# Softmax split over three engines, fewer fill-in products and operands built chunk by chunk in a fused attention and feed-forward kernel

## The chip, the cores and the metric

The kernel runs on 1 core of one Trainium2 chip. The metric is the device time of one launch in microseconds. All operands are 32-bit floats in memory.

## What is computed

The reference is sparse attention, then a mixture of 8 experts with Sinkhorn-balanced weights, then a feed-forward block with an ELU. Only the attention and the first product of the experts bear on the change.

```python
B, H, S, D = 4, 8, 576, 64; stride = 32
scores = q @ k.T / sqrt(D)                       # per batch and head
mask_local   = (rel >= 0) & (rel < 32)           # heads 0 to 3
mask_strided = (rel >= 0) & (i % 32 == j % 32)   # heads 4 to 7
scores = where(mask, scores, -1e9)
attn = exp(scores - max(scores)); attn /= sum(attn) + 1e-9
x = (attn @ v)  as  (B*S, H*D) = (2304, 512)
P = sinkhorn(exp(x @ w_gate - max))              # 8 iterations
for e in range(8): out += P[:, e] * (relu(x @ w1[e]) @ w2[e])
result = elu(out @ w_in) @ w_out
```

## The kernel before, in words

**Attention.** Heads are taken in pairs, batch by batch: 16 pairs `m`, and each pair in two halves, so 32 units `u`. A unit is one score tile set: 5 or 4 tiles of 128x96 in a pair of local heads, 6 or 5 tiles of 108x54 in a pair of strided heads. The order of pairs in a batch is local, strided, local, strided. A unit passes four stages, which are generators in `attention()` (L683). `att_s1` (L415) transposes q and k by chunks on PE; ACT copies q into the block operand `q_blk` (L437), DVE copies k into `kT` (L443). `att_s2` (L453) has the score products (L470), the mask add on DVE (L484), the maximum on DVE (L487); the exponentials (L491, one activation per tile, each with the tile's row sum) and the normalisation (L495 to L497: two small DVE operations, then a multiplication on POOL, GpSimd's row in the profile) are put off. `att_s3` (L503) transposes the weights on PE (L511), and DVE or ACT copies them to `eT` (L514, L516). `att_s4` (L519) multiplies by v (L529) and DVE copies the result to x (L549).

**Order.** The kernel writes the order of each engine's instructions by hand. In one round of `attention()` the stages of several units are called in the order s2(u), s1, s4(u-3), s1, s3(u-2), s3(u-2), and after each call `tick()` counts down the operations that are put off: `DEF_EXP = 3` and `DEF_NORM = 5` say after how many calls. After a call in the first stage one step of a build (`build_step`) or of the weights' preparation (`prep_step`) is issued too. Each engine runs its instructions in that order.

**Fill-in products.** While attention runs alone, `warm_up` (L337) adds a 128x512 product of constants (L341) to the first nine PSUM banks and then to every second one (`WARM_MOD = 2`). Its result is overwritten.

**First operands.** The experts' first product runs on 1024 tokens by a scheme of seven products (Strassen-Winograd). Its seven right operands are B11, B21 (`build_a`, L247) and T2, T1, T3, T4, B22 (`build_b`, L255), each of 2 chunks of 128 rows by 512 tokens, each split into a high and a low part: ACT casts the high one, DVE or POOL subtracts for the low one (`low`, L167). T1 to T4 are differences that DVE takes first (L267). `build_a` starts when batch 0 is done and `build_b` when batch 1 is done (`batch_done`, L634), each with both chunks.

**Where attention alone ends.** At round 21 (`MOE_FROM`) the experts' first product (`gemm1`, L969, products at L925) begins on PE, and the rest of attention is spread between its steps. `need` (L678) issues the rest of a build that a product needs. The gate (`gate_block`, L577, products L589) waits in PE's order for the same operands. From about 230 us to the end at 2067 us the kernel is the experts' products (L925, L1074).

Of the kernel before, what the change touches and what calls it, by code (L numbers as in the profile page):

```python
# [24 lines left out]
KD = DM // P  # L25
# [50 lines left out]
def sparse_attention_moe_kernel(ctx: ExitStack, tc: tile.TileContext, a, out):  # L76
# [170 lines left out]
    def build_a(src):  # L247

        hi, lo = xb
        for x, c0 in ((B11, 0), (B21, 2)):  # L250
            yield from splits([(hi[:, x, c], lo[:, x, c], src(c + c0), ve if c else po_) for c in (0, 1)])
            built.add(x)
            yield True

    def build_b(a, b, home=None):  # L255


        hi, lo = xb

        def minus(x, y, i, c):  # L260
            if home:
                out = home(i, c)
            elif i == 4:
                out = y
            else:
                out = hp_.tile([P, HALF], F32, tag="hh" if c else "hl", name="t")
            ve.tensor_tensor(out=out, in0=x, in1=y, op=ALU.subtract)  # L267
            return out

        t1 = [minus(b(c), a(c), 1, c) for c in (0, 1)]  # L270
        yield True
        t2 = [minus(b(c + 2), t1[c], 2, c) for c in (0, 1)]
        yield True

        def both(x, t, engs):
            for c in (0, 1):
                se.copy(hi[:, x, c], t[c])
            yield True
            for c in (0, 1):
                low(hi[:, x, c], lo[:, x, c], t[c], engs[c])  # L280
            built.add(x)
            yield True

        yield from both(T2, t2, (ve, ve))
        yield from both(T1, t1, (ve, po_))
        t3 = [minus(t2[c], a(c), 3, c) for c in (0, 1)]
        yield from both(T3, t3, (ve, po_))

        t4 = [minus(a(c + 2), t2[c], 4, c) for c in (0, 1)]
        yield from both(T4, t4, (ve, po_))  # L290
        b22 = [b(c + 2) for c in (0, 1)]
        yield from both(B22, b22, (ve, ve))
# [160 lines left out]
    def att_s2(u):  # L453
# [11 lines left out]
        for i, x in enumerate(tiles):  # L465
            if local:
                qc, kc = x * P, max(0, x * LQ - STRIDE)
            else:
                qc, kc = x * 2 * NJ, x * NJ
            pe.matmul(  # L470
                pp[:nq, i * nk : (i + 1) * nk],
                q_blk[m % 2][:, qc : qc + nq],
                t["kT"][:, kc : kc + nk],
                start=True,
                stop=True,
            )
# [10 lines left out]
        ve.tensor_reduce(out=ng, in_=e, axis=AX.X, op=ALU.max, negate=True)  # L487

        def exps():
            for i in range(nt):  # L490
                se.activation(e[:, i], e[:, i], AF.Exp, bias=ng[:, i : i + 1], accum_out=sm[:, i : i + 1])  # L491

        def norm():
            rc = st_p.tile([P, 6], F32, tag="rc", name="rc")[:nq, :nt]
# [8 lines left out]
    def att_s3(u):  # L503
# [3 lines left out]
        for i0 in (0, 3):  # L507
# [5 lines left out]
            if i0 and not local:  # L513
                se.copy(dst, pt[:nk, : n * nq])  # L514
            else:
                ve.tensor_copy(dst, pt[:nk, : n * nq])  # L516
# [60 lines left out]
    def gate_block():  # L577

        for half, parts in enumerate((((B11, 0), (B21, 2)), ((B11, 0), (T1, 0), (B22, 2)))):
            while not all(x in built for x, _ in parts):  # L580
                yield True
# [52 lines left out]
    def batch_done(b):  # L634

        if b == 0:
            po_.tensor_copy(x1_[:, :, : S - HALF], x0_[:, :, HALF:])
            start_build((0, False, "a"), build_a(lambda c: x0_[:, c, :HALF]))
            gates.append(gate_block())
        elif b == 1:  # L640
            start_build((0, False, "b"), build_b(lambda c: x0_[:, c, :HALF], lambda c: x1_[:, c, :HALF]))
            gates.append(gate_tile(NA // P, x1_[:, :, HALF:]))

    def pair_done(m):

        b, hp = pair_of(m)
        t0 = max(NA, b * S)
# [30 lines left out]
    def need(x):  # L678
        while x not in built:
# [3 lines left out]
    def attention():  # L683
# [4 lines left out]
        for u in range(NU + 5):  # L688
# [5 lines left out]
            if u - 5 == 2 * H:  # L694
                batch_done(1)
# [19 lines left out]
            if w == H - 1:  # L715
                batch_done(0)
# [252 lines left out]
    def gemm1(sg, p, early=False):  # L969
# [6 lines left out]
        def prod(dst, wi, xi, start=True):  # L976
            need(xi)
            for c in products(dst, w, xb, wi, xi, start=start):
# [311 lines left out]
WARM0, WARM1, WARM_MOD, WARM_OF, WARM_N = 14, 10, 2, 1, 512  # L1290
QK_BUFS = 3
DEF_EXP, DEF_NORM = 3, 5
# [35 lines left out]
```

## Time and profile before

| | |
|---|---|
| median of 3 runs | 2068.71 us (2067.12 to 2068.77) |
| profiled execution, its own time | 2068.94 us |
| its span | 2067.2 us |
| TensorE (PE) busy | 2029.2 us, 98% |
| VectorE (DVE), ScalarE (ACT), GpSimd (POOL) busy | 1306.3, 743.4, 633.8 us |
| mean granted clock of TensorE | 0.989 |

The profile's times are microseconds from the span's start. The profiled execution's own time stands 1.7 us over its span, and 0.2 us over the median. A busy PE need not be at its full rate: PEclk is the share of the full clock (2.4 GHz) that was granted, so 0.50 is 1.2 GHz. In a timeline, the first number is the start, the second the length, and brackets give the idle time ahead of it with what ended it. Matmuls overlap, so the distance between two starts is the price of one, not its length.

### The profile page before, as it was taken

The page shows a single profiled execution, that of the slowest core. Times are in us where ns is not written, and L with a number is a line of the kernel's source. Part 1 is how long each engine was busy: PE and PEld are TensorE (multiplying, and loading weights), DVE is VectorE, ACT ScalarE, POOL GpSimd, SP SyncE. Part 2 cuts the span into 40 slices and gives each one's busy share as a digit, 9 for nine tenths or more (in the row PEclk, how much of TensorE's full clock was granted, in tenths as well). Part 3 has the DMA queues.
Part 4 walks back from the last instruction along what each step waited for, and adds up shares of the span by engine and source line. Part 5 has one row for each costly group of instructions (what it writes and reads, how often), then busy time and mean ns, then how long its engine had stood idle before and what let it go on. Part 6 is the DMA issues. An engine that isn't in the chain of part 4 may idle for free.

```text
span 2067.2 us, 26959 instructions
## 1 busy us (share of the span) xinstructions
PE 2029.2 (98%) x10196; PEld 1681.0 (81%) x10196; DVE 1306.3 (63%) x2165; ACT 743.4 (36%) x1707; POOL 633.8 (31%) x709
## 2 busy tenths in 40 slices
PE   9889999999999999999999999999999989999999
PEld 7767778888888888788888888888888878887887
DVE  6767766555555546566666676766665475558665
ACT  7656233223222323322222222222222254445543
POOL 2422333333332324322222222222222222224240
PEclk9899999999999999999999999999999999999999
DMA  9632111111111113222222222222221101122111
GB/s 195 132 72 73 68 52 61 41 52 62 52 41 52 61 51 101 73 83 81 75 84 72 84 75 80 79 74 85 72 77 46 42 21 42 41 82 92 42 51 51
DMA packets 143378, 143.12 MB, mean 69 GB/s; under 512 B 67328, under 2 KB 106128, under 8 KB 143248
## 3 DMA queue, kind: packets, MB, share of 16 engines
q1 hardware_dynamic: 142288, 141.20, 23.0%
q8 instruction: 80, 1.31, 0.3%
q14 instruction: 50, 0.41, 0.1%
q10 hardware_dynamic: 960, 0.21, 0.1%
HBM read 123.55 MB, written 20.19 MB: 70 GB/s over the span
## 4 chain that ended last, share of the span: by engine, by line
PE 90%; DVE 5%; ACT 4%; issue 1%; POOL 0%; DVEq 0%; ACTq 0%; POOLq 0%
PE ybank L1074 46%; PE bank L925 39%; DVE xl L168 1%; PE ybank L529 1%; ACT g L948 1%; PE bank L470 1%; ACT g L947 1%; DVE u L984 1%; PE ybank L511 1%; ACT e_t L491 1%; PE ybank L470 1%; ACT hh L952 0%; PE bank L425 0%; ACT q_blk L437 0%; DVE rawa L267 0%
## 5 line engine op out<-in xcount | busy, mean ns | idle before, releaser
L1074 PE MATMUL ybank<-w2h,hh 128*128 128x512 f32 x1280 | 502.7, 393 | 1.5 <-ACT q_blk L437 0.8
L1074 PE MATMUL ybank<-w2h,hl 128*128 128x512 f32 x1280 | 498.3, 389 | 0.0
L1074 PE MATMUL ybank<-w2l,hh 128*128 128x512 f32 x1280 | 498.2, 389 | 0.0
L925 PE MATMUL bank<-xh,w1h 128*128 128x512 f32 x1120 | 446.6, 399 | 16.3 <-DVE u L984 7.8
L925 PE MATMUL bank<-xl,w1h 128*128 128x512 f32 x1120 | 440.0, 393 | 6.1 <-DVE xl L168 6.1
L925 PE MATMUL bank<-xh,w1l 128*128 128x512 f32 x1120 | 438.6, 392 | 0.0
L168 POOL TENSOR_TENSOR w1l<-w1raw,w1h 128x256 fp32r<-128x256 f32 x240 | 207.8, 886 | 438.4 <-ACT w1h L158 438.3
L1105 DVE SCALAR_TENSOR_TENSOR acc<-ybank,prob,acc 128x512 f32<-128x512 f32 x244 | 182.7, 749 | 231.4 <-PE ybank L1074 231.0
L1074 PEld LDWEIGHTS ybank<-w2h,hh 128*128 128x128 f32 x1280 | 240.3, 188 | 52.7 <-DVE acc L1091 1.9
L1074 PEld LDWEIGHTS ybank<-w2h,hl 128*128 128x128 f32 x1280 | 240.2, 188 | 50.3
L1074 PEld LDWEIGHTS ybank<-w2l,hh 128*128 128x128 f32 x1280 | 240.4, 188 | 48.1
L168 POOL TENSOR_TENSOR w2l<-w2raw,w2h 128x512 fp32r<-128x512 f32 x80 | 104.1, 1302 | 564.8 <-ACT w2h L158 549.5
L158 ACT CAST w2h<-w2raw 128x512 fp32r<-128x512 f32 x160 | 97.4, 622 | 476.3 <-issue 396.1
L925 PEld LDWEIGHTS bank<-xh,w1h 128*128 128x128 f32 x1120 | 211.8, 189 | 67.0 <-DVE u L984 11.1
L925 PEld LDWEIGHTS bank<-xl,w1h 128*128 128x128 f32 x1120 | 212.1, 189 | 47.0 <-DVE xl L168 7.8
L925 PEld LDWEIGHTS bank<-xh,w1l 128*128 128x128 f32 x1120 | 211.9, 189 | 45.1
L984 DVE TENSOR_TENSOR u<-bank,a 128x512 f32<-128x512 f32 x160 | 110.5, 691 | 194.8 <-PE bank L925 163.5
L186 POOL TENSOR_TENSOR wsum<-w1raw 128x256 f32<-128x256 f32 x160 | 125.3, 783 | 216.0 <-DMA w1raw<-in_moe_w 149.4
L940 ACT ACTIVATE hh<-bank 128x512 fp32r<-128x512 f32 x192 | 114.1, 594 | 106.8 <-DVE bank L984 104.0
L942 DVE SCALAR_TENSOR_TENSOR hl<-bank,hh 128x512 fp32r<-128x512 f32 x192 | 131.3, 684 | 6.3
L168 DVE TENSOR_TENSOR w1l<-wsum,w1h 128x512 fp32r<-128x512 f32 (+1 forms) x164 | 119.2, 735 | 13.7 <-ACT w1h L158 12.7
L940 ACT ACTIVATE hh<-c 128x512 fp32r<-128x512 f32 x64 | 40.6, 634 | 242.7 <-DVE c L984 242.7
(198 smaller groups left out, 2707.1 us busy)
## 6 DMA issues: line engine op xcount, KB each, us to landing
w1raw<-in_moe_w SPq DMA_DIRECT2D x64, 512.0 KB, 3.4
w2raw<-in_moe_w SPq DMA_DIRECT2D x64, 512.0 KB, 3.5
raw<-in_moe_w_in SPq DMA_DIRECT2D x16, 512.0 KB, 3.8
w_conv<-val SPq DMA_DIRECT2D x32, 256.0 KB, 2.5
raw<-in_moe_w_out SPq DMA_DIRECT2D x16, 512.0 KB, 3.7
w1raw<-w_conv SPq DMA_DIRECT2D x16, 512.0 KB
w2raw<-w_conv SPq DMA_DIRECT2D x16, 512.0 KB, 3.4
q_t<-in_q SPq DMA_DIRECT2D x32, 144.0 KB, 3.9
```

What stands on the lines that cost most here:

```text
L158: se.copy(hi, src)
L168: eng.tensor_tensor(out=lo, in0=src, in1=hi.bitcast(F32), op=ALU.subtract)
L186: po_.tensor_tensor(out=o, in0=x, in1=y, op=op)
L470: pe.matmul(pp[:nq, i * nk : (i + 1) * nk], q_blk[m % 2][:, qc : qc + nq], t["kT"][:, kc : kc + nk], start=True, stop=True,)
L491: se.activation(e[:, i], e[:, i], AF.Exp, bias=ng[:, i : i + 1], accum_out=sm[:, i : i + 1])
L511: pe.transpose(pt[:nk, i * nq : (i + 1) * nq], s["e"][:, i0 + i], ident[:nq, :nq])
L925: pe.matmul(dst, a_[:, wi, c, :], b_[:, xi, c, :], start=start and i == 0, stop=stop and i == 5, skip_group_check=True,)
L940: se.activation(hh, src, AF.Relu)
L942: ve.scalar_tensor_tensor(out=hl, in0=src, scalar=0.0, in1=hh.bitcast(F32), op0=ALU.max, op1=ALU.subtract)
L984: ve.tensor_tensor(out=out, in0=x, in1=y, op=ALU.add)
L1074: pe.matmul(y, x[:, cs], w[:, f], start=first and f + m == 0, stop=last and f == 1 and m == 2)
L1105: ve.scalar_tensor_tensor(out=at, in0=y, scalar=prob[:, g, e : e + 1], in1=at, op0=ALU.mult, op1=ALU.add)
```

## The change

The softmax of a unit is spread otherwise. The maximum is kept with its own sign, POOL subtracts it from all tiles in one operation, ACT takes one exponential over all tiles, and DVE sums the rows in the normalisation, which is put off by one more call. ACT makes all copies to `eT`. Fill-in products follow every eighth bank. `build_a` and `build_b` take the chunks one at a time: chunk 0 of `build_a` starts when the second pair of batch 0 is done, chunk 1 with the fourth; the same for `build_b` in batch 1. A product waits for the chunk that it reads.

```diff
-    def build_a(src):
+    def build_a(src, cs=(0, 1)):
...
-            yield from splits([(hi[:, x, c], lo[:, x, c], src(c + c0), ve if c else po_) for c in (0, 1)])
-            built.add(x)
+            yield from splits([(hi[:, x, c], lo[:, x, c], src(c + c0), ve if c else po_) for c in cs])
+            built.update((x, c) for c in cs)
...
-    def build_b(a, b, home=None):
+    def build_b(a, b, home=None, cs=(0, 1)):
...
-        t1 = [minus(b(c), a(c), 1, c) for c in (0, 1)]
+        t1 = {c: minus(b(c), a(c), 1, c) for c in cs}
...
-        ve.tensor_reduce(out=ng, in_=e, axis=AX.X, op=ALU.max, negate=True)
+        ve.tensor_reduce(out=ng, in_=e, axis=AX.X, op=ALU.max)
+        po_.tensor_tensor(out=e, in0=e, in1=ng[:, :, None].to_broadcast([nq, nt, nk]), op=ALU.subtract)
 
         def exps():
-            for i in range(nt):
-                se.activation(e[:, i], e[:, i], AF.Exp, bias=ng[:, i : i + 1], accum_out=sm[:, i : i + 1])
+            se.activation(e, e, AF.Exp)
 
         def norm():
+            ve.tensor_reduce(out=sm, in_=e, axis=AX.X, op=ALU.add)
...
-            if i0 and not local:
-                se.copy(dst, pt[:nk, : n * nq])
-            else:
-                ve.tensor_copy(dst, pt[:nk, : n * nq])
+            se.copy(dst, pt[:nk, : n * nq])
...
-            start_build((0, False, "a"), build_a(lambda c: x0_[:, c, :HALF]))
...
-            start_build((0, False, "b"), build_b(lambda c: x0_[:, c, :HALF], lambda c: x1_[:, c, :HALF]))
...
     def pair_done(m):
 
         b, hp = pair_of(m)
+        if b < 2 and m % 2:
+
+            cs = (m % KD // 2,)
+            if b:
+                start_build("b", build_b(lambda c: x0_[:, c, :HALF], lambda c: x1_[:, c, :HALF], cs=cs))
+            else:
+                start_build("a", build_a(lambda c: x0_[:, c, :HALF], cs))
...
-    def need(x):
-        while x not in built:
+    def need(x, c=0):
+        while (x, c) not in built:
...
-            need(xi)
-            for c in products(dst, w, xb, wi, xi, start=start):
+            work = products(dst, w, xb, wi, xi, start=start)
+            for c in (0, 1):
+                need(xi, c)
+                next(work)
                 if c == 0:
                     gap()
...
-WARM0, WARM1, WARM_MOD, WARM_OF, WARM_N = 14, 10, 2, 1, 512
+WARM0, WARM1, WARM_MOD, WARM_OF, WARM_N = 14, 10, 8, 1, 512
...
-DEF_EXP, DEF_NORM = 3, 5
+DEF_EXP, DEF_NORM = 3, 6
```

In the order of instructions this looks as follows at three places. First DVE, one round in the middle of attention alone (`e_t` are a unit's scores, `ng` the maxima, `sm` the row sums, `rc` their inverse, `acc` holds x), before:

```order
L484 TENSOR_TENSOR e_t<-bank,m_local 128x384
L487 TENSOR_REDUCE ng<-e_t 128x4
L549 COPY acc<-ybank 128x18x18
L443 COPY kT<-bank 128x9x32
L516 COPY eT<-ybank 54x324
L495 TENSOR_SCALAR rc<-sm 128x4
L496 RECIPROCAL rc<-rc 128x4
```

and with the change:

```order
L479 TENSOR_TENSOR e_t<-bank,m_local 128x384
L482 TENSOR_REDUCE ng<-e_t 128x4
L489 TENSOR_REDUCE sm<-e_t 128x5
L491 TENSOR_SCALAR rc<-sm 128x5
L492 RECIPROCAL rc<-rc 128x5
L542 COPY acc<-ybank 128x18x18
L443 COPY kT<-bank 128x9x32
```

The copy to `eT` has gone to ACT; the normalisation is now that of the unit before (128x5 behind the maximum of 128x4) and has a sum of its own.

Second PE, the same stretch of attention alone, before:

```order
L529 MATMUL ybank<-eT,v_t 64x64 x10
L425 MATMUL bank<-ident,k_t 128x96 x3
L341 MATMUL ybank<-warm 128x512
L511 MATMUL ybank<-ident,e_t 96x128 x4
L341 MATMUL bank<-warm 128x512
L470 MATMUL bank<-kT,q_blk_110 128x96 x5
L425 MATMUL bank<-ident,q_t 128x96 x3
L341 MATMUL ybank<-warm 128x512
L529 MATMUL ybank<-eT,v_t 64x64 x8
```

and with the change:

```order
L522 MATMUL ybank<-eT,v_t 64x64 x10
L425 MATMUL bank<-ident,k_t 128x96 x3
L507 MATMUL ybank<-ident,e_t 96x128 x4
L471 MATMUL bank<-kT,q_blk_110 128x96 x5
L425 MATMUL bank<-ident,q_t 128x96 x3
L341 MATMUL ybank<-warm 128x512
L522 MATMUL ybank<-eT,v_t 64x64 x8
```

Two of three fill-in products are gone here; over the whole stage there are 21 in place of 60 (the 14 at the very start stay).

Third DVE around the first product of the experts, whose first mask add from a `ybank` marks the place (`t` are the differences of `build_b`, `xl` the low parts), before:

```order
L484 TENSOR_TENSOR e_t<-ybank,m_str 108x270
L487 TENSOR_REDUCE ng<-e_t 108x5
L267 TENSOR_TENSOR t<-acc 128x512 x2
L267 TENSOR_TENSOR t<-acc,t 128x512 x2
L549 COPY xlate<-ybank 128x320
L443 COPY kT<-ybank 128x288
L168 TENSOR_TENSOR xl<-t,xh 128x512 x2
```

and with the change:

```order
L479 TENSOR_TENSOR e_t<-ybank,m_str 108x270
L482 TENSOR_REDUCE ng<-e_t 108x5
L489 TENSOR_REDUCE sm<-e_t 108x6
L491 TENSOR_SCALAR rc<-sm 108x6
L492 RECIPROCAL rc<-rc 108x6
L267 TENSOR_TENSOR t<-acc 128x512
L267 TENSOR_TENSOR t<-acc,t 128x512
L542 COPY xlate<-ybank 128x320
L443 COPY kT<-ybank 128x288
L168 TENSOR_TENSOR xl<-t,xh 128x512
```

Only chunk 1 is left here. Chunk 0 of `build_b`, 4 differences and 5 low parts on DVE, has moved ahead, into the last rounds of attention alone.

## Rows read from the trace of the kernel before

**Rows 1.** The page's 40 slices: PE's busy time in tenths.

```profile
PE   9889999999999999999999999999999989999999
```

**Rows 2.** Busy time by engine in five stretches: us, PE, PEld, DVE, ACT, POOL, PEclk, DMA.

```profile
20.59:54.00 33.41, 32.95 (x397) 28.48 (x395) 26.19 (x71) 27.84 (x116) 8.51 (x12) 1.00 1.03 201
...
30.05:45.02 14.97, 14.75 (x181) 12.72 (x177) 11.71 (x32) 12.31 (x51) 3.20 (x5) 1.00 0.94 213
...
54.00:90.42 36.42, 33.32 (x310) 28.66 (x308) 25.82 (x59) 26.32 (x98) 14.43 (x17) 0.77 0.58 120
...
62.84:77.97 15.13, 15.13 (x100) 13.01 (x99) 7.86 (x19) 8.40 (x39) 4.37 (x5) 0.50 0.63 127
...
90.42:147.94 57.52, 49.21 (x334) 34.25 (x331) 40.71 (x83) 30.55 (x100) 21.20 (x20) 0.91 0.44 94
```

**Rows 3.** PE's timeline: fill-ins at either clock, and starts after idle time.

```profile
15.98 1.70 PE L470 MATMUL bank<-kT,q_blk 128*108 128x54 f32 x12 [2.26 <-ACT q_blk L437]
...
30.05 0.47 PE L425 MATMUL bank<-ident,k_t 96*128 96x96 f32 x3
...
38.72 0.48 PE L341 MATMUL bank<-warm 128*128 128x512 f32 x1
39.04 1.25 PE L470 MATMUL bank<-kT,q_blk 128*128 128x96 f32 x10
...
61.38 1.53 PE L529 MATMUL ybank<-eT,v_t 54*64 54x54 f32 x24 [2.16 <-DVE eT L516]
...
71.59 0.78 PE L341 MATMUL bank<-warm 128*128 128x512 f32 x1
72.16 1.91 PE L470 MATMUL bank<-kT,q_blk 128*108 128x54 f32 x10
...
102.54 0.50 PE L925 MATMUL bank<-xl,w1h 128*128 128x512 f32 x1 [1.91 <-DVE xl L168]
...
118.16 0.50 PE L925 MATMUL bank<-xl,w1h 128*128 128x512 f32 x1 [2.26 <-DVE xl L168]
```

**Rows 4.** DVE by line and shape, 0 to 90.42 us: count, busy us, mean ns.

```profile
L516 DVE COPY eT<-ybank 96x384 f32<-96x384 f32 x8 | 4.4, 554 | 2.1 <-PE ybank L511 1.6
...
L487 DVE TENSOR_REDUCE ng<-e_t 128x5 f32<-128x480 f32 x5 | 3.3, 655 | 0.2
...
L487 DVE TENSOR_REDUCE ng<-e_t 108x5 f32<-108x270 f32 x4 | 1.7, 436 | 0.1
...
L516 DVE COPY eT<-ybank 96x128 f32<-96x128 f32 x4 | 1.1, 278 | 0.0
```

**Rows 5.** ACT's timeline at unit 0: the first of its five exponentials, then `q_blk`.

```profile
12.59 0.38 ACT L491 ACTIVATE e_t<-e_t,ng 128x96 f32<-128x96 f32 x1
...
14.52 1.36 ACT L437 ACTIVATE q_blk<-bank 64x288 f32<-64x288 f32 x2
```

**Rows 6.** ACT by line and shape, 0 to 90.42 us: casts of 512 and of 256 elements.

```profile
L158 ACT CAST xh<-acc 128x512 fp32r<-128x512 f32 x4 | 2.5, 616 | 0.0
...
L158 ACT CAST w1h<-wsum 128x256 fp32r<-128x256 f32 x4 | 1.6, 397 | 0.0
```

**Rows 7.** POOL by line and shape, 0 to 90.42 us: largest and smallest multiplication.

```profile
L497 POOL TENSOR_TENSOR e_t<-e_t,rc 128x480 f32<-128x480 f32 x5 | 5.0, 990 | 24.5 <-DVE rc L496 14.0 <-ACT eT L514 7.4 <-DVE e_t L484 3.1
...
L497 POOL TENSOR_TENSOR e_t<-e_t,rc 108x270 f32<-108x270 f32 x4 | 2.6, 640 | 11.2 <-DVE rc L496 5.4 <-PE bank L470 3.8 <-ACT xh L158 1.9
```

**Rows 8.** Timelines of POOL (first and last of four operations in a row) and DVE.

```profile
56.18 1.27 POOL L168 TENSOR_TENSOR xl<-acc,xh 128x512 fp32r<-128x512 f32 x1
...
58.78 0.74 POOL L186 TENSOR_TENSOR wsum<-w1raw,wsum 128x256 f32<-128x256 f32 x1
...
56.68 3.39 DVE L168 TENSOR_TENSOR xl<-acc,xh 128x512 fp32r<-128x512 f32 x1
```

**Rows 9.** Line 168 on DVE, 0 to 240 us: min/median/max ns.

```profile
L168 DVE TENSOR_TENSOR xl<-t,xh x5: 681/693/1222, 97.4 to 112.0; 128x512 fp32r<-128x512 f32 x5
```

**Rows 10.** PE's waits, 90 to 320 us: total us, times, longest.

```profile
PE bank L925 <- DVE xl L168: 6.1, 5, 2.3
```

More of the change, by code (lines that the diff above doesn't have):

```diff
@@ L268, in minus @@
             return out
-        t1 = [minus(b(c), a(c), 1, c) for c in (0, 1)]
+        t1 = {c: minus(b(c), a(c), 1, c) for c in cs}
         yield True
-        t2 = [minus(b(c + 2), t1[c], 2, c) for c in (0, 1)]
+        t2 = {c: minus(b(c + 2), t1[c], 2, c) for c in cs}
         yield True
         def both(x, t, engs):
-            for c in (0, 1):
+            for c in cs:
                 se.copy(hi[:, x, c], t[c])
             yield True
-            for c in (0, 1):
+            for c in cs:
                 low(hi[:, x, c], lo[:, x, c], t[c], engs[c])
-            built.add(x)
+                built.add((x, c))
             yield True
@@ L285, in build_b @@
         yield from both(T1, t1, (ve, po_))
-        t3 = [minus(t2[c], a(c), 3, c) for c in (0, 1)]
+        t3 = {c: minus(t2[c], a(c), 3, c) for c in cs}
         yield from both(T3, t3, (ve, po_))
-        t4 = [minus(a(c + 2), t2[c], 4, c) for c in (0, 1)]
+        t4 = {c: minus(a(c + 2), t2[c], 4, c) for c in cs}
         yield from both(T4, t4, (ve, po_))
-        b22 = [b(c + 2) for c in (0, 1)]
+        b22 = {c: b(c + 2) for c in cs}
         yield from both(B22, b22, (ve, ve))
@@ L469, in att_s2 @@
                 qc, kc = x * 2 * NJ, x * NJ
[L470 to L476, printed above, removed]
+            dst = pp[:nq, i * nk : (i + 1) * nk]
+            pe.matmul(dst, q_blk[m % 2][:, qc : qc + nq], t["kT"][:, kc : kc + nk], start=True, stop=True)
         s3 = pp[:nq, : nt * nk].rearrange("p (t k) -> p t k", k=nk)
@@ L579, in gate_block @@
         for half, parts in enumerate((((B11, 0), (B21, 2)), ((B11, 0), (T1, 0), (B22, 2)))):
-            while not all(x in built for x, _ in parts):
+            while not all((x, c) in built for x, _ in parts for c in (0, 1)):
                 yield True
@@ L693, in attention @@
             s2, s3, s4 = of(att_s2, u - 2), of(att_s3, u - 4), of(att_s4, u - 5)
-            if u - 5 == 2 * H:
-                batch_done(1)
             for gen in (s2, s1, s4, s1, s3, s3):
@@ L714, in attention @@
                 reorder_v(u // 8 + 1, H // 4 + RE_IN.index(u % 8))
-            if w == H - 1:
-                batch_done(0)
+            if w == H - 1 or w == 2 * H - 1:
+                batch_done(w // H)
     load_qk(0)
```

## The prediction

> **What bounds it now.** I start with the slices of the page: PE is busy in nearly all of them [rows 1], so only two things can bring time: PE work that disappears, and the few places where PE idles or runs at the lower clock. From about 230 us on the kernel is not touched by the change. So I read the first 150 us by stretches [rows 2]. In 20.59 to 54.00 nine units of attention pass, 33.41/9 = 3.71 us each; PE is busy 32.95 of it at full clock, so PE sets the pace there, although DVE (26.19) and ACT (27.84) are not far below. In 54.00 to 90.42 seven units take 5.2 us each, and the granted clock is 0.77: PE waited 2.16 us ahead of 61.38 [rows 3] and then ran at 0.50 (1.2 GHz) from 62.84 to 77.97. The same piece of program lies between 30.05 and 38.72 at full clock [rows 3]: 8.67 us against 15.13, so the lower clock cost 6.5 us. In 90.42 to 147.94 the experts' first product has begun; PE is busy only 49.21 of 57.52, and the clock is 0.91. What it waited for is above all low parts of its right operands [rows 10], which DVE makes too late.
>
> A look at the idle times ahead of clock losses: 2.26, 2.16 and 2.26 us were followed by the lower clock, 1.91 us was not [rows 3]. [...]
>
> **The change, part by part.** For the softmax I use the steady stretch 30.05 to 45.02, four units in 14.97 us [rows 2].
>
> *PE.* A fill-in at full clock costs 38.72 to 39.04, 0.32 us [rows 3]. In four units there are 24 banks, so 12 fill-ins before and 3 after: 9 x 0.32 = 2.9 us. PE idles 14.97 - 14.75 = 0.2 us here. PE's floor is then 14.97 - 0.2 - 2.9 = 11.9 us, 2.97 a unit.
>
> *DVE.* It loses the copies to `eT`, six in four units, between 0.278 and 0.554 us each [rows 4], some 2.7 us (most are of the longer kinds); it gains four row sums, which read what the maxima read: 0.436 to 0.655 [rows 4], together 2.1. So 11.71 - 2.7 + 2.1 = 11.1 us, 2.8 a unit: below PE, but by little.
>
> *ACT.* Five exponentials with their sums held ACT from 12.59 to 14.50, 1.9 us [rows 5]; four units have 20 of them, at most 7.6 us, and as the strided tiles are narrower I take 7.2. One exponential over 270 to 480 elements isn't in the trace; the nearest rows are casts, 0.397 for 256 and 0.616 for 512 [rows 6], so 0.4 to 0.6, four of them 2.0. With the six copies (about 2.7): 12.31 - 7.2 + 2.0 + 2.7 = 9.8 us. ACT gets room.
>
> *POOL.* The subtraction has the shapes of the multiplication: 0.640 to 0.990 [rows 7], so 3.2 more on 3.20 us [rows 2], 6.4 of 12. It is behind the maximum in POOL's order, and what is queued behind it (weights' low parts, the multiplication of the unit before) waits for that maximum. It lengthens a unit's own chain, but the sum is wanted only a round later, behind the next maximum; there I cost it at nothing. POOL needs 1.27 us for a low part that DVE makes in 0.693 [rows 8, 9]. On DVE the four subtractions would cost about 2.2 us (as the maxima) and raise its floor to 13.3, over PE's. The Trainium skill ("GPSIMD Engine Reference", section 4.1) says that elementwise work belongs on VectorE, GpSimd being about twice as slow for two inputs; the ratio agrees with the rows, and by that rule the stage would end at DVE's 13.3 us; since POOL has the room, the sum goes by POOL.
>
> So a unit is bounded by 2.97 below and today's 3.71 above (the copies to `eT`, the value product and the next transposes follow each other closely, and DVE is nearly full). I take 3.2, nearer to the floor, because PE was 99% busy in the rows with slower neighbours. **Term 1**, nine units: 9 x 3.2 - 33.4 = -4.6 us (0 to -6.7).
>
> **Term 2, the start.** Unit 0's exponentials hold the `q_blk` copies until 14.52 [rows 5], PE waits for them until 15.98 and then has the lower clock for about 4 us [rows 3]. Now POOL's subtraction (0.99) and one exponential (0.6) follow the maximum, which was there before the first exponential at 12.59 [rows 5]: the copies start by 14.2 at the latest, 0.3 us earlier, and up to 0.6 more if the maximum had been there for some time (ACT had come from other copies). I take 0.9. PE also gets there sooner, so its wait may still be near 2 us; the clock I leave as it is (if it holds, -1.7 more). -1 (0 to -2.6).
>
> **Term 3, the last seven units of attention alone** (36.42 us). Here the builds run. PE's floor is 7 x 2.97 = 20.8, but DVE now gets chunk 0 of `build_b`: 4 differences and 5 low parts at about 0.69 [rows 9], 6.2 us. DVE: 25.82 [rows 2] - 1.1 (softmax, 7/4 of 0.6) + 6.2 = 30.9 us, so DVE becomes the engine that sets the pace. With about 2 us of its own waits 33: -3.4 us. Ends: 30.9 (-5.5), and 36.4 (0), about what PE needs if the clock stays at half: without fill-ins the stretch at half clock is 15.13 - 7 x 0.57 [rows 3] = 11.1 us against 8.67 - 7 x 0.32 = 6.4 at full, a factor 1.7, and 7 x 2.97 x 1.7 = 35.
>
> **Term 4, the first product of the experts** (57.52 us). PE idles 8.3 us. The clock's 0.91 is 0.09 x 57.5 x 2 = 10.4 us at half, which cost 10.4 x (1 - 1/1.7) = 4.3. Half of the operands are now there, and each product reads chunk 0 first. DVE has 6.2 us less here. I take 4.5 of the idle time and, as no 2 us wait should be left, 3 of the clock: -7.5 (0 to -12.6). The weights' preparation and the gate stay where they are behind it. What comes after, 13 units between the experts' products, has ACT relieved and POOL loaded, and PE there has no idle time worth a term: 0.
>
> Sum: -4.6 - 1 - 3.4 - 7.5 = -16.5 us on the profiled execution's 2068.94: **2052.4**. The median lies 0.2 lower: 2052.
>
> **Rivals.**
>
> *The clock falls and stays (ends slower).* Fewer fill-ins leave PE with more short waits, DVE and PE being within 0.8 us in four units; one 2 us wait early, and PE runs at 1.2 GHz with little to raise it. A unit is then 2.97 x 1.7 = 5.05 us. In all 17 units from 15.98 on, the experts begin at 102, 11.5 us later than now, and term 4 gives only the 4.5 of idle time: +7, 2076 us. Each of the ten early units at the lower clock costs 1.85 against my 3.2, each of the last seven, which DVE paces, 0.35. So with the last seven and term 4 without their clock it decides from 6 of the ten early units on, and from 8 on the kernel is measurably slower. For it: after 61.38 the clock stayed low for 16 us, with fill-ins. Against: at full clock PE stays the busiest engine, and a 1.91 us wait did no harm.
>
> *DVE waits for POOL.* At 56.68 a low part on DVE took 3.39 us instead of 0.69: it ended when four operations of POOL in a row (56.18 to 59.52) had ended [rows 8], and then PE stood 2.16 us. POOL now has an operation more per unit. Some 24 DVE operations of that kind (2 + 9 + 6 of the builds, 7 of the weights) run until about 130 us; if half of them meet one more subtraction of 0.8 us: +9.6, 2062 us. By the Trainium skill ("SBUF — State Buffer", section "Who interferes with whom") a VectorE instruction with two inputs in SBUF and a GpSimd instruction that reads SBUF exclude each other for a whole instruction, and a reduction never takes part. The trace agrees, and the wait outlasted four instructions, not one; mask adds (one PSUM operand) and sums would be spared.
>
> *The change moves work and wins nothing.* The unit stays at 3.71 because its chain of copies and products sets it, not PE's fill-ins; chunk 0 costs its 6.2 us ahead of the experts' product, and term 4 gives 7.5 back. Start 0. Together -1.3: 2067.6. For it: ACT and DVE had 0.78 to 0.83 of the steady stretch. Against: PE's 99%.
>
> **How the numbers follow.** Forecast (2042 to 2059): 0.62. DVE behind POOL, 2062: 0.18, faster too. Nothing won, 2067.6: 0.10, the same. Clock, 2076: 0.10, of which I give 0.02 to "same" because it may last for fewer units. A measurement tells 0.2%, 4 us, from no change. Faster 0.80, same 0.12, slower 0.08. All terms at their ends give 2041.5; the range goes from 2041 to 2067, which leaves out the clock case and part of the others.
>
> **What the profile would show.** Right: four steady units in 12 to 13 us with PE over 0.9 busy at clock 1.00; the experts' first product at about 81 us instead of 90.4; waits for `xl` there at most half of 6.1 us; DVE fullest in the last rounds before. Wrong: PEclk of 0.5 in several of the first slices; DVE operations of line 168 over 1.5 us; steady units at 3.7 us with PE idle between them; or waits for the subtraction ahead of the exponentials that come through to PE.

## The result, and the profile after

The changed kernel takes 2085.32 us (median of 5 runs, 2081.02 to 2086.54), the kernel before 2068.77 us on the same chip: ratio 1.0073 [1.0056, 1.0091], slower by 0.7%, where 2052 was forecast. Its profiled execution took 2084.83 us, 15.9 more than that of before. From the page, PE's busy time, its slices and its clock:

```profile
PE 2035.8 (98%) x10157; PEld 1691.1 (81%) x10157; DVE 1310.4 (63%) x2149; ACT 717.2 (34%) x1467; POOL 659.5 (32%) x741
...
PE   8789999999999999999999999999999989999999
...
PEclk7679999999999999999999999999999999999999
```

PE is busier than before (2035.8 against 2029.2 us) with 39 products fewer: the same work ran at a lower clock, and the loss lies in the first three slices, some 156 us. Five stretches of the changed kernel by engine (columns as in [rows 2]):

```profile
14.29:108.13 93.84, 78.42 (x691) 71.01 (x692) 62.53 (x137) 46.59 (x102) 37.69 (x46) 0.65 0.64 132
35.77:56.25 20.48, 18.41 (x167) 16.67 (x168) 12.37 (x29) 10.27 (x22) 8.84 (x10) 0.67 0.66 147
56.25:79.28 23.03, 18.41 (x167) 16.67 (x168) 15.53 (x31) 11.25 (x25) 10.07 (x14) 0.65 0.53 112
79.28:102.62 23.34, 19.03 (x168) 17.17 (x168) 17.89 (x38) 12.08 (x28) 9.98 (x12) 0.65 0.37 76
108.13:166.21 58.08, 51.50 (x333) 37.09 (x331) 36.26 (x73) 23.26 (x51) 23.20 (x26) 0.84 0.39 88
```

The experts begin at 108.13 instead of 90.42 us, 17.7 later; the mean clock up to there is 0.65. Their first product takes 58.08 us (57.52 before), and what comes behind it takes 2.4 us less (1916.9 us from 166.21 to the span's end, 1919.3 from 147.94 before). So attention alone holds the whole loss. The second to fourth rows are rounds of four units: the first of them takes 20.48 us, 5.12 a unit, where four units took 14.97 before [rows 2]. Where a round begins is read from PE's timeline, at starts with idle time ahead:

```profile
14.29 2.23 PE L471 MATMUL bank<-kT,q_blk 128*108 128x54 f32 x12 [1.74 <-ACT q_blk L437]
19.83 1.30 PE L507 MATMUL ybank<-ident,e_t 128*96 128x128 f32 x5 [2.33 <-POOL e_t L493]
32.26 0.91 PE L522 MATMUL ybank<-eT,v_t 54*64 54x54 f32 x24 [0.60 <-ACT eT L509]
35.77 2.38 PE L471 MATMUL bank<-kT,q_blk 128*108 128x54 f32 x12 [1.48 <-DVE kT L443]
56.25 2.38 PE L471 MATMUL bank<-kT,q_blk 128*108 128x54 f32 x12 [1.48 <-DVE kT L443]
79.28 2.38 PE L471 MATMUL bank<-kT,q_blk 128*108 128x54 f32 x12 [4.02 <-DVE kT L443]
96.96 1.19 PE L522 MATMUL ybank<-eT,v_t 54*64 54x54 f32 x24 [0.90 <-ACT eT L509]
102.62 2.38 PE L471 MATMUL bank<-kT,q_blk 128*108 128x54 f32 x12 [3.35 <-ACT eT L509]
```

PE waits at the first unit of each strided pair: three times for `kT`, at 14.29 for `q_blk`, at 102.62 for `eT`. And the clock round such a place, in windows of four microseconds:

```profile
32.00:36.00 4.00, 2.25 (x35) 1.89 (x35) 3.52 (x8) 3.00 (x7) 1.98 (x3) 0.87 1.31 244
36.00:40.00 4.00, 4.00 (x36) 3.67 (x36) 1.67 (x4) 0.81 (x2) 0.55 (x1) 0.50 0.21 32
40.00:44.00 4.00, 4.00 (x22) 3.80 (x22) 1.27 (x5) 1.22 (x3) 1.00 (x2) 0.50 0.26 76
44.00:48.00 4.00, 4.00 (x35) 3.66 (x34) 2.57 (x7) 2.40 (x6) 2.60 (x3) 0.50 0.50 113
48.00:52.00 4.00, 4.00 (x46) 3.65 (x45) 2.85 (x7) 2.37 (x4) 0.99 (x1) 0.93 1.05 316
52.00:56.00 4.00, 2.18 (x35) 1.63 (x33) 3.90 (x9) 3.47 (x8) 3.58 (x4) 0.93 1.18 191
```

At 0.50 PE is the bound (4.00 of 4.00) and the others wait for it. When the clock rises, PE runs ahead, DVE is full (3.52, 3.90 of 4.00), PE waits, the clock is 0.50 again. What DVE does just ahead of `kT`, from its timeline, and POOL's subtractions of the same microseconds:

```profile
30.34 0.81 DVE L491 TENSOR_SCALAR rc<-sm 108x5 f32<-108x5 f32 x1
...
32.70 0.55 DVE L482 TENSOR_REDUCE ng<-e_t 128x4 f32<-128x384 f32 x1
33.17 0.64 DVE L489 TENSOR_REDUCE sm<-e_t 128x5 f32<-128x480 f32 x1
33.84 0.43 DVE L491 TENSOR_SCALAR rc<-sm 128x5 f32<-128x5 f32 x1
34.31 0.19 DVE L492 RECIPROCAL rc<-rc 128x5 f32<-128x5 f32 x1
34.41 0.67 DVE L542 COPY acc<-ybank 128x324 f32<-128x324 f32 x1
34.93 0.69 DVE L443 COPY kT<-bank 128x288 f32<-128x288 f32 x1
```

```profile
30.14 0.99 POOL L483 TENSOR_TENSOR e_t<-e_t,ng 128x480 f32<-128x480 f32 x1 [3.92 <-PE bank L425]
...
33.42 0.83 POOL L483 TENSOR_TENSOR e_t<-e_t,ng 128x384 f32<-128x384 f32 x1 [1.26 <-DVE ng L482]
```

The norm (sum, addition, reciprocal) stands between a maximum and the copies that release PE: from 33.17 to 34.41, 1.24 us longer to `kT`. And the addition of `EPS` to five numbers a row takes 0.43 and 0.81 us: both times it ends with POOL's subtraction (30.34 + 0.81 and 30.14 + 0.99; 33.84 + 0.43 and 33.42 + 0.83). In the kernel before it took 0.16 to 0.17 us, by shape (count, busy us, mean ns, 0 to 90.42 us):

```profile
L495 DVE TENSOR_SCALAR rc<-sm 108x5 f32<-108x5 f32 x4 | 0.7, 165 | 0.4 <-ACT e_t L491 0.4
```

The wait of 4.02 us ahead of 79.28 has one thing more ahead of it: a low part on DVE, 0.65 us at its shortest, took 2.65 and ended 0.5 us behind the last of four operations of POOL in a row (72.49 to 75.19). From DVE's and POOL's timelines:

```profile
73.08 2.65 DVE L168 TENSOR_TENSOR xl<-acc,xh 128x512 fp32r<-128x512 f32 x1
...
74.47 0.72 POOL L186 TENSOR_TENSOR wsum<-w1raw,wsum 128x256 f32<-128x256 f32 x1
```

### The profile page after: what moved, and what is told of

Read it like the earlier page. It is cut to its first block, busy times and chain, and to the rows that moved or that the text cites. A ratio compares the mean times of both kernels' runs of the same rounds, so it can differ in the third digit from the quotient of the medians.

```text
span 2083.1 us, 26678 instructions
## 1 busy us (share of the span) xinstructions
PE 2035.8 (98%) x10157; PEld 1691.1 (81%) x10157; DVE 1310.4 (63%) x2149; ACT 717.2 (34%) x1467; POOL 659.5 (32%) x741
## 4 chain that ended last, share of the span: by engine, by line
PE 89%; DVE 7%; ACT 3%; issue 1%; POOL 0%; DVEq 0%; POOLq 0%; ACTq 0%
PE ybank L1072 45%; PE bank L921 38%; PE bank L471 1%; DVE xl L168 1%; PE ybank L522 1%; ACT g L944 1%; PE ybank L507 1%; ACT g L943 1%; PE ybank L471 1%; DVE u L982 1%; PE bank L425 1%; DVE e_t L479 0%; DVE ng L482 0%; ACT hh L948 0%; DVE rc L491 0%
## 5 line engine op out<-in xcount | busy, mean ns | idle before, releaser
L921 PEld LDWEIGHTS bank<-xh,w1h 128*128 128x128 f32 x1120 | 212.0, 189 | 68.0 <-DVE u L982 11.2
L168 DVE TENSOR_TENSOR w1l<-wsum,w1h 128x512 fp32r<-128x512 f32 (+1 forms) x164 | 121.1, 746 | 13.9 <-ACT w1h L158 12.9
```

Of the source, the lines that this page charges most:

```text
L168: eng.tensor_tensor(out=lo, in0=src, in1=hi.bitcast(F32), op=ALU.subtract)
L921: pe.matmul(dst, a_[:, wi, c, :], b_[:, xi, c, :], start=start and i == 0, stop=stop and i == 5, skip_group_check=True,)
```

## The experiments

Theories after the result: A, the fill-ins left out explain it; B, the new softmax does (the norm and its addition on DVE's way to `kT`). "Experts" is the start of their first product in the profiled execution, "clock" PE's mean granted clock from 14 us to there. The names say how a kernel differs from the one before or from the changed one ("after"). The ratio is to runs of the kernel before on the same chip, whose medians lie between 2068.0 and 2068.7 us. The profiled execution lies at or near one end of the range in after_fill2 (2075.5 us), chunks_fill8 (2077.5), chunks_fill2_n128 (2067.8), after_fill_strided (2069.3) and chunks_strided (2071.0), so there the last two columns do not stand for the median.

| run | median us (range) | ratio to before [interval] | experts | clock |
|---|---|---|---|---|
| before, after | 2068.77, 2085.32 | 1.0073 [1.0056, 1.0091] | 90.4, 108.1 | 0.87, 0.65 |
| after_fill2 | 2080.26 (2075.54 to 2083.71) | 1.006 [1.0037, 1.0083] | 103.1 | 0.80 |
| before_fill8 | 2075.53 (2068.02 to 2083.47) | 1.0035 [1.0015, 1.0055] | 99.8 | 0.69 |
| before_chunks | 2058.94 (2058.27 to 2059.05) | 0.9957 [0.9941, 0.9974] | 87.1 | 0.92 |
| before_softmax | 2078.18 (2069.29 to 2080.86) | 1.0045 [1.0031, 1.0059] | 95.1 | 0.85 |
| fill2_norm5 | 2063.02 (2057.88 to 2068.06) | 0.9967 [0.9953, 0.998] | 88.6 | 0.89 |
| fill2_norm9 | 2069.03 (2067.33 to 2072.17) | 1.0002 [0.9992, 1.0012] | 90.5 | 0.86 |
| fill2_noeps | 2072.11 (2066.11 to 2073.09) | 1.0016 [1.0004, 1.0028] | 99.0 | 0.82 |
| norm5_oldcopy | 2066.75 (2062.44 to 2069.76) | 0.999 [0.9979, 1.0001] | 92.9 | 0.87 |
| chunks_actcopy | 2059.01 (2055.6 to 2065.48) | 0.9955 [0.994, 0.997] | 88.8 | 0.91 |
| after_norm5 | 2072.45 (2068.07 to 2075.82) | 1.0022 [1.0008, 1.0035] | 98.4 | 0.69 |
| chunks_fill8 | 2072.68 (2068.36 to 2077.46) | 1.002 [1.0006, 1.0033] | 104.6 | 0.62 |
| chunks_fill1 | 2067.16 (2066.07 to 2068.52) | 0.9991 [0.9981, 1.0] | 93.9 | 0.96 |
| chunks_fill8x4 | 2057.27 (2056.04 to 2058.84) | 0.9951 [0.9936, 0.9966] | 83.1 | 0.95 |
| chunks_fill2_n128 | 2077.08 (2067.45 to 2081.19) | 1.0038 [1.002, 1.0055] | 95.9 | 0.74 |
| after_fill_strided | 2072.66 (2069.33 to 2078.67) | 1.0029 [1.0015, 1.0044] | 96.9 | 0.83 |
| after_fill_local | 2084.42 (2082.93 to 2091.56) | 1.0089 [1.0071, 1.0107] | 111.3 | 0.70 |
| chunks_strided | 2064.11 (2061.75 to 2070.95) | 0.9981 [0.9968, 0.9993] | 98.0 | 0.82 |
| norm5_fill8x4 | 2057.92 (2055.95 to 2058.57) | 0.9947 [0.9929, 0.9965] | 85.3 | 0.92 |

### The parts of the change apart

after_fill2 sets the fill-ins back; before_fill8 makes that step alone; before_chunks takes only the new `build_a`, `build_b` and what calls them; before_softmax only the softmax, the later norm and the copies on ACT.

```diff
-WARM0, WARM1, WARM_MOD, WARM_OF, WARM_N = 14, 10, 8, 1, 512
+WARM0, WARM1, WARM_MOD, WARM_OF, WARM_N = 14, 10, 2, 1, 512
```

> The changed kernel with fill-in products at every second bank again (60 instead of 21). Theory A (the fill-ins are what is missing: PE runs ahead of DVE, waits about 2 us in every second pair, and the clock drops to 1.2 GHz for some 13 us each time): PE works through those waits, PEclk in attention alone is 0.85 or more instead of 0.65, a unit takes 3.4 to 3.8 us instead of 5.1, the experts' products begin at 80 to 90 us instead of 108, time 2055 to 2065. Theory B (the softmax chain over POOL and the longer row of DVE operations ahead of the copy to kT sets the pace, at any clock): a unit stays at 4.5 us or more, the experts begin after 100, time 2075 to 2086.

> The kernel before with fill-in products at every eighth bank, nothing else. Theory A: PE now outruns ACT and DVE here too, waits, and the clock drops: PEclk in attention alone at 0.65 to 0.75, the experts begin at 100 to 107 us, time 2078 to 2086. Theory B: without the new softmax PE's waits are short, the clock holds as before, the experts begin by 88 us, time 2060 to 2069.

> The kernel before with the operands built chunk by chunk, softmax and fill-ins as before. My fourth term: the experts' products begin at 92 to 97 us (chunk 0 adds 6.2 us to DVE in the last rounds), PE waits less for xl behind that (3 instead of 6.1 us), time 2058 to 2066. The rival (the work is only moved): the experts begin 6 us later and the waits shrink by no more than that, time 2067 to 2071.

> The kernel before with the new softmax (subtraction on POOL, one exponential, sums on DVE, copies to eT on ACT, normalisation one call later), both chunks built together, 60 fill-ins. Theory A: a unit takes 3.3 to 3.7 us, the clock holds as before, the experts begin at 82 to 90 us, time 2060 to 2068. Theory B: a unit takes over 4.2 us with PE waiting for kT, the experts begin after 98 us, time 2075 or more.

Each part was put into the kernel before by itself. Against that kernel's 2068.0 us on the same chip the chunks win 9.1 us (within the 2058 to 2066 expected), the split softmax costs 10.2 and the missing fill-ins cost 7.5. A falls, since after_fill2 keeps 12.3 us of the loss; B alone falls too, since fewer fill-ins cost something without the split (before_fill8 lies between the two ranges expected of it). The parts do not add up: their sum is +8.6 us, the whole change costs 16.6. With the split softmax as it stands the chunks win nothing (before_softmax 2078.2, after_fill2 2080.3). Two expectations of the experts' start missed: 87.1 us in before_chunks instead of 92 to 97, and 95.1 in before_softmax, where B had it after 98. PE's waits for parts of right operands from the experts' begin to 340 us (total, times, longest), first in before_chunks, then in the changed kernel:

```profile
PE bank L923 <- POOL xl L168: 1.5, 2, 0.8
...
PE bank L923 <- ACT xh L277: 0.6, 2, 0.4
PE bank L923 <- DVE xl L168: 0.6, 2, 0.4
```

```profile
PE bank L921 <- DVE xl L168: 2.0, 2, 1.2
PE bank L921 <- ACT xh L277: 1.9, 1, 1.9
PE bank L921 <- POOL xl L168: 1.6, 2, 1.3
```

[Rows 10] had 6.1 us for DVE's low parts. With chunks alone the stretch from 87.06 to 138.5 takes 51.44 us instead of 57.52, and these rows add up to 2.7 us. In the changed kernel they add up to 5.5, and the clock is 0.84 instead of 0.91.

### Where in the softmax

All on after_fill2: the norm one call earlier (fill2_norm5) or three later (fill2_norm9), or without the addition of `EPS` (fill2_noeps). In fill2_norm9 the last unit and half of the last but one are transposed before their division, so that their weights stay undivided.

```diff
-DEF_EXP, DEF_NORM = 3, 6
+DEF_EXP, DEF_NORM = 3, 5
```

```diff
-            ve.tensor_scalar_add(rc, sm, EPS)
-            ve.reciprocal(rc, rc)
+            ve.reciprocal(rc, sm)
```

> The same kernel with the norm one tick earlier instead, ahead of the next unit's mask, as it stood in the kernel before: the tiny addition no longer meets GpSimd's subtraction, and the chain from the scores to kT is that of before; but the sums come sooner behind the one exponential. Theory C: waits for kT under 3 us, 2058 to 2068 us. Rival D: 2074 us or more, with VectorE waiting ahead of the sums for ScalarE's exponential (which itself waits for GpSimd).

> The changed kernel with fill-in products at every second bank again (as in the run before, which took 2080.3 us) and the three VectorE operations of the norm (sum, addition, reciprocal) issued three scheduler ticks later, that is behind the output copy and the copy of kT instead of ahead of them. Theory C (the loss of the softmax part is VectorE's chain to kT, 1.5 to 1.7 us longer by the norm that stands between the maximum and kT; TensorE waits there and its clock falls): TensorE's waits for kT shrink from 6.0 to under 3 us, the experts begin before 92 us instead of 103.1, and the run takes 2058 to 2066 us. Rival D (GpSimd's subtraction and the shared port set the pace of the units, wherever the norm stands): 2074 us or more, waits for kT or e_t stay near 6 us.

> The changed kernel with fill-in products at every second bank, and the addition of EPS to the sums left out (the reciprocal reads the sums; the output differs in the last digits). It prices the addition that ends with GpSimd's subtraction, 0.41 to 0.81 us each time. If the port wait belongs to that operation, VectorE's chain to kT is 0.4 to 0.8 us shorter per unit and the run is 3 to 8 us faster than 2080.3, with the experts begun before 100 us. If the wait moves to the reciprocal (which then takes 0.4 us or more instead of 0.19), nothing is won: 2077 us or more.

One number moves 17.2 us (2080.3 to 2063.0). DVE's timeline of fill2_norm5 shows the way to `kT` without the norm, and the additions by shape (count, busy us, mean ns, 0 to 100 us) there and in after_fill2:

```profile
29.74 0.56 DVE L482 TENSOR_REDUCE ng<-e_t 128x4 f32<-128x384 f32 x1
30.21 0.73 DVE L542 COPY acc<-ybank 128x324 f32<-128x324 f32 x1
30.77 0.71 DVE L443 COPY kT<-bank 128x288 f32<-128x288 f32 x1
31.88 0.55 DVE L489 TENSOR_REDUCE sm<-e_t 128x4 f32<-128x384 f32 x1 [0.41 <-ACT e_t L486]
```

```profile
L491 DVE TENSOR_SCALAR rc<-sm 108x5 f32<-108x5 f32 x4 | 0.9, 216 | 0.1
```

```profile
L491 DVE TENSOR_SCALAR rc<-sm 108x5 f32<-108x5 f32 x4 | 3.2, 812 | 0.1
```

The addition falls from 812 to 216 ns, and PE's waits for `kT`, 1.15, 1.16 and 3.72 us in after_fill2, are 0.62, 0.63 and 0.95. Leaving the addition out (fill2_noeps) gains 8.2 us, and the reciprocal that then follows the sum does not inherit its wait:

```profile
L491 DVE RECIPROCAL rc<-sm 108x5 f32<-108x5 f32 x4 | 0.8, 190 | 0.1
```

So the addition's wait for POOL is about half of the norm's cost (8.2 of 17.2 us); that the rest is its place follows only if the two add up, which no run shows. Theory C holds, D falls. fill2_norm9 has the shortest way to `kT` (one wait of 0.8) but wins only 11.2, a miss of its 2058 to 2066: PE still waits 1.6 us for POOL's multiplication (1.7 in after_fill2), and 2.8 for `eT`.

The rest of the softmax: `eT` copies as before on fill2_norm5 (norm5_oldcopy), and those copies alone on before_chunks (chunks_actcopy).

```diff
-            se.copy(dst, pt[:nk, : n * nq])
+            if i0 and not local:
+                se.copy(dst, pt[:nk, : n * nq])
+            else:
+                ve.tensor_copy(dst, pt[:nk, : n * nq])
```

> The changed kernel with fill-in products at every second bank and the norm at five (2063.0 us), and the copies of eT back where they were (VectorE's, except the second of a strided unit). It asks what is left of the 4 us to the run with chunks alone (2058.9). If it is the copies on ScalarE: 2058 to 2060 us. If it is GpSimd's subtraction and the one exponential behind it: 2062 us or more; VectorE then has both the sums and the copies, some 1 us more in a unit, and 2066 us would say that VectorE is what is short.

> The kernel before with building by chunks and, of the softmax part, only the copies of eT moved from VectorE to ScalarE; the maximum subtracted in ScalarE's exponentials, one for each tile, as before. If relief of VectorE helps by itself: 2053 to 2058 us, with waits for kT under the 2.7 us of the run with chunks alone. If ScalarE, with four to six exponentials each unit and now all copies, becomes late with eT: 2061 us or more, and waits for eT over 2 us.

With the sums on DVE, its copies cost 3.7 us (the two intervals just touch), which speaks for DVE as what is short in the split. Without the split, moving the copies changes nothing (2059.0 against 2058.9); neither of the two expected outcomes came.

### What the fill-ins do

after_norm5 is the changed kernel with the norm at five; chunks_fill8 and chunks_fill1 are before_chunks with `WARM_MOD` 8 and 1.

> The changed kernel (2085.3 us) with one number set back: the norm five ticks behind the scores instead of six, so that sum, addition and reciprocal stand ahead of the next unit's mask and not between its maximum and the copy of kT. Fill-in products stay at every eighth bank. Theory C (what costs is the norm's place on VectorE's chain to kT; with the chain short again TensorE doesn't wait and few fill-ins are enough): 2055 to 2065 us, the experts begun before 92 us instead of 108.1. Theory E (the norm's place and the fill-ins each cost something of their own, since with the chain short there are still waits of 1 to 2 us after which the clock falls): 2066 to 2074 us.

> The kernel before with building by chunks alone (2058.9 us) and fill-in products at every eighth bank. Theory E (fewer fill-ins cost some 7 us whatever the builds do, as with the kernel before): 2064 to 2069 us. If fewer fill-ins only hurt where xl is late, which building by chunks has mended: 2050 to 2059 us, since 60 fewer products at 0.21 to 0.43 us are 9 to 12 us of TensorE's own work.

> The kernel before with the building by chunks alone (2058.9 us) and fill-in products at every bank of units 0 to 13 (WARM_MOD 1) instead of every second. If the clock in attention is what is still lost there (0.77 and 0.83 in the stretches 80:100 and 100:120 of that run, 1.00 before 80), more fill-ins change little ahead of 80 us: each costs 0.21 us at the high clock, some 60 more, so 0 to +8 us: 2058 to 2067. If fill-ins are cheap beside the waits that they fill, as the run with fewer of them (+7.5 us) suggests, it gains up to 3 us: 2055 to 2059.

Fewer fill-ins cost 9.4 us with the norm at five (theory E) and 13.7 with chunks alone, more than the 7 expected; twice as many cost 8.2. The windows of chunks_fill8, and of before_chunks:

```profile
16.00:48.00 32.00, 32.00 (x232) 29.36 (x232) 17.45 (x46) 19.07 (x83) 6.02 (x7) 0.50 0.70 139
```

```profile
16.00:48.00 32.00, 30.83 (x336) 26.57 (x337) 22.85 (x61) 26.97 (x110) 9.41 (x11) 0.95 1.02 200
```

This was the surprise: behind the start's wait (2.5 us) PE is busy 32.00 of 32.00 us and stays at 0.50 throughout, with no further wait. So waits aren't all: what the fill-ins give back is the clock, and 232 products pass where 336 did (4 and 24 of them fill-ins). Two runs take amount and spacing apart, with four fill-ins at each eighth bank, and with 128 columns instead of 512 at each second.

```diff
-            pe.matmul(t[:, :WARM_N], warm[:, :P], warm[:, :WARM_N], start=True, stop=True)
+            for _ in range(1 if n_banks[0] < WARM1 else 4):
+                pe.matmul(t[:, :WARM_N], warm[:, :P], warm[:, :WARM_N], start=True, stop=True)
```

```diff
-            pe.matmul(t[:, :WARM_N], warm[:, :P], warm[:, :WARM_N], start=True, stop=True)
+            w = WARM_N if n_banks[0] < WARM1 else 128
+            pe.matmul(t[:, :w], warm[:, :P], warm[:, :w], start=True, stop=True)
```

> Chunk builds alone with fill-in products at every eighth bank, but four of them there: as many as at every second bank (2058.9 us), lumped. With one at every eighth bank the run took 2072.7 us and the clock was 0.50 from 16 to 48 us although TensorE never stood idle there. If the number counts and not the spacing: 2056 to 2062 us, experts begun before 89 us. If the spacing counts, or the lumps delay the copies behind them: 2065 us or more.

> Chunk builds alone with fill-in products at every second bank, but of 128 columns instead of 512 past the first ten: a quarter of the work, as at every eighth bank (2072.7 us), spaced as at every second (2058.9). If the amount of fill-in work counts: 2068 us or more, with the clock near 0.5 in the stretch 16 to 48 us. If the spacing counts: under 2058 us, since some 50 products then cost a quarter of 0.21 us each.

In lumps they are worth as much as spaced (2057.3 and 2058.9 us), and as many of 128 columns are worth nothing (2077.1): here their amount counted, not their spacing. The clock near 0.5 that was expected of chunks_fill2_n128 did not show: it was 0.84 from 16 to 48 us, though in an execution of 2067.8 us, and seven of its nine took 2073.9 to 2081.2. Then the place, with six products added in the changed kernel at each of the four units ahead of which PE waits, three times for `kT` and once for `eT` (after_fill_strided), or at four where it doesn't (after_fill_local, `local` in place of `not local`); chunks_strided puts twelve at the former into chunks_fill8.

```diff
         pp = warm_up(abank())
+        if alone_now[0] and m > 1 and hf == 0 and not local:
+            for _ in range(6):
+                pe.matmul(pp[:, :WARM_N], warm[:, :P], warm[:, :WARM_N], start=True, stop=True)
```

> The changed kernel (2085.3 us) with six more fill-in products (128x512) ahead of the score products of the first unit of each strided pair from the fourth pair on while attention is alone (24 in all): the place where TensorE waited 1.5, 1.5, 4.0 and 3.4 us at 35.77, 56.25, 79.28 and 102.62 us, after which the granted clock was 0.50 for some 13 us. Theory W (those waits bring the clock down): with the waits filled the clock stays at 1.00 behind these places, TensorE's clock between 36 and 79 us rises from 0.66 to over 0.85, the experts begin before 99 us instead of 108.1, 2067 to 2076 us. Theory N (it is how much or how often fill-in products run, wherever): about what the next run gives.

> The same 24 fill-in products, in the same count of places, but ahead of the score products of the first unit of each local pair, where TensorE did not wait for kT. Theory W: they fill nothing there; at 0.21 to 0.43 us each they cost 5 to 10 us or delay the next wait by as much: 2083 to 2092 us. Theory N: as good as the run with them at the strided pairs, within 4 us, and both under 2080 us, since 24 of the 60 removed products are back.

> Chunk builds alone with one fill-in product at every eighth bank (2072.7 us) and twelve more ahead of the score products of the first unit of each strided pair from the fourth pair on (48). It asks whether the place counts by itself: as many products as lumped at every eighth bank (2057.3 us), at four places 20 units apart. If a stretch of fill-ins at the place of the wait is enough to hold the clock: 2054 to 2062 us. If the clock falls again in the units between: 2064 us or more.

The same 24 products win 12.7 us where PE waits and 0.9, nothing that can be told, where it doesn't. Windows from 28 to 68 us of the first and of the second kernel:

```profile
28.00:68.00 40.00, 35.63 (x431) 30.78 (x430) 34.14 (x74) 26.10 (x55) 21.55 (x27) 1.00 0.83 167
```

```profile
28.00:68.00 40.00, 35.84 (x343) 31.81 (x343) 25.18 (x59) 19.45 (x42) 15.95 (x20) 0.76 0.61 133
```

With the waits of 1.48 us filled the clock is 1.00 for 40 us. In the second kernel both of these waits remain, and behind each the clock falls to 0.50 (from 40 to 48 and from 60 to 68 us). So theory W holds for the changed kernel: those waits bring the clock down. In the first kernel PE's next wait, 2.62 us for `kT` ahead of 68.85, is longer than its fill-ins, and from 72 to 80 us the clock is 0.50 again. chunks_strided, at 2064.1, falls just into the second outcome expected of it (2064 or more): 48 more products at four places win 8.6 us over chunks_fill8, where 36 more in lumps at every eighth bank win 15.4. With chunks alone, then, filling these places is not enough. (Its expectation says places "20 units apart"; they are four units apart.)

### Nothing but the sound parts

norm5_fill8x4 is after_norm5 with the lumped fill-ins.

> The changed kernel with the norm at five and the fill-in products lumped, four at every eighth bank: all parts of the change but the two that the runs so far found costly (the norm behind the next maximum, a quarter of the fill-in products). With one at every eighth bank it took 2072.5 us, with one at every second 2063.0. If both costs are settled by these two numbers: 2055 to 2063 us, and the split softmax is worth nothing beside chunk builds alone (2057.3 lumped). If the split softmax wins once neither is in its way, as the prediction had it: under 2055 us.

It is 0.5% faster than the kernel before, and no faster than chunks_fill8x4 without the split softmax (2057.9, 2057.3). These two are the best found here; the split softmax is worth nothing that these runs can tell.

## Why the prediction was wrong

**The step that failed** is in the paragraph on POOL: the sum "is wanted only a round later, behind the next maximum; there I cost it at nothing". What the norm was put in front of, on DVE, is the copies of the output and of `kT`, and PE stands at the strided pair's first unit until `kT` is there. Setting the norm back alone moves 12.9 us (after to after_norm5) or 17.2 (with fill-ins).

**DVE's sum was too small.** Forecast 11.1 us in four units, measured 12.37 (first round above). The additions explain it: 0.81, 0.41, 0.38 and 0.41 us in the four shapes against 0.16 to 0.17 before, 1.35 us. With that, DVE passes PE's forecast floor of 11.9. I had said that sums and mask adds would be spared; they were, and I overlooked the addition between them. The Trainium skill ("SBUF — State Buffer", section "Who interferes with whom") counts `tensor_scalar` among the operations that can use the pair of ports shared with GpSimd, with the whole operation as the lock; the 0.81 and 0.43 us that end with POOL's subtraction agree. So the rival of DVE waiting for POOL came in through an operation that it did not count, and once as forecast, in the 2.65 us of line 168.

**The fill-ins were booked as pure gain**, 2.9 us in four units. Without them PE had the lower clock: +7.5, +9.4 and +13.7 us in the three pairs with the norm ahead of the mask, +5.1 with it behind (after_fill2 to after). Setting both back, the norm and the fill-ins, moves 22.3 us (after to fill2_norm5); no run shares out the 11 us from there to the forecast, and the terms below say what is known of them.

**Term 1, -4.6.** Even at full clock it isn't there: after_fill_strided takes 15.16 us for four units (fill-ins at 34.26 and 49.42), norm5_fill8x4 takes 15.04 (30.95 to 45.99), the kernel before 14.97 [rows 2]. In the first of these there are nine fill-ins in four units, and PE is busy 14.17 us. The floor of 11.9 supposes three of them and the full clock together, and no run has both: with three in four units the mean clock was 0.67 (changed kernel, first round) and 0.50 (chunks_fill8). What the split would take at the full clock without the others stays open. In its number this is the rival "moves work and wins nothing".

**Term 2, -1.** The start came 1.7 us earlier (14.29 instead of 15.98), but a wait of 2.33 us for POOL's multiplication followed at 19.83, and the mean clock from 14.29 to 28.29 was 0.51.

**Terms 3 and 4** come out nearly right with chunks alone: the experts begin 3.4 us earlier (forecast 3.4) and their first product takes 6.1 us less (forecast 7.5). For term 3 that is luck, since before_chunks has neither fewer fill-ins nor the split softmax; what it gains there is that the wait of 2.16 us ahead of 61.38 [rows 3] is gone and the clock is 1.00 from 54 to 76 us. In term 4 the idle time fell as forecast, from 8.3 to 3.9 us, but the 3 us of clock were mis-sized: the mean clock is 0.91 in both kernels, and PE's busy time fell by 1.6. In the changed kernel term 3's stretch was lost to the clock and the waits, and term 4 gave nothing back.

Term 4 took its 3 us because no wait of 2 us should be left. No run shows such a bound. In the kernel before itself the clock was 0.50 again 2 us behind a wait of 0.67 us, with very small products between (16x16 and 128x8):

```profile
127.29 0.42 PE L565 MATMUL ybank<-ident,lg 16*128 16x16 f32 x4 [0.67 <-ACT lg L593]
...
129.68:132.53 2.85, 2.85 (x11) 2.18 (x10) 2.23 (x6) 0.78 (x3) 0.00 (x0) 0.50 1.10 291
```

And the length of the wait alone does not tell: among few fill-ins 0.61 us was followed by the lower clock (before_fill8, first two lines), among sixty 1.15 us was not (after_fill2):

```profile
33.25 2.38 PE L470 MATMUL bank<-kT,q_blk 128*108 128x54 f32 x12 [0.61 <-DVE kT L443]
33.25:45.00 11.75, 11.75 (x88) 10.88 (x89) 6.17 (x17) 6.29 (x31) 1.56 (x2) 0.50 0.46 90
...
36.14 1.31 PE L471 MATMUL bank<-kT,q_blk 128*108 128x54 f32 x12 [1.15 <-DVE kT L443]
36.14:48.00 11.86, 11.86 (x139) 10.53 (x140) 8.53 (x22) 7.11 (x15) 5.39 (x7) 1.00 0.69 169
```

**Sizes** that held: one exponential 0.43 to 0.60 us (0.4 to 0.6), POOL's subtraction 0.64 to 0.99, ACT 10.27 us in four units (9.8).

**The rival that came true** is the clock: 5.05 us a unit forecast; 5.12, 5.76 and 5.84 measured in the three rounds; experts at 102, in fact 108.1. That 5.12 is so near is chance: the rival had PE at half clock throughout, and in these rounds it ran at 0.65 to 0.67 and stood idle for 2.1 to 4.6 us. I gave the rival 0.10 on two grounds that were wrong: that PE would stay the busiest engine at full clock, and that a wait of 1.91 us did no harm [rows 3]; here waits of 1.48 us were followed by the lower clock.

## What to carry to other kernels

When an operation is moved, write down what stands behind it in its engine's order and who waits for that; a place costs as much as a duration. Products that do nothing but keep TensorE's clock are priced by a run without them, not by their own length. A change of several parts is measured part by part: here one part won 9.1 us and two others lost more than it, and together they lost more than the sum of the parts.

## What the runs showed of the hardware

TensorE stayed at 1.2 GHz for 32 us with its records showing no idle time (chunks_fill8, 16 to 48 us), and in attention waits of 1.48 us (changed kernel) and 0.61 us (before_fill8) were followed by the lower clock, while one of 1.15 us among more fill-ins (after_fill2) was not. Fill-in products of 128x512 gave a mean clock of 0.95 in lumps of four and 0.92 singly up to the experts' begin (chunks_fill8x4, before_chunks), as many of 128 columns 0.74 (chunks_fill2_n128). How the clock is judged is left open. An addition over 108x5 elements on DVE took 0.81 us beside a GpSimd subtraction (0.165 in the kernel before), a reciprocal in its place 0.19. A subtraction of 128x512 on DVE, 0.65 us at its shortest, took 2.65 beside four GpSimd operations in a row.
